# Scores of a windowed attention: every unit by plain float32 products on two row halves of the tensor engine

## The chip, the cores and the metric

The kernel runs on one core of a Trainium2 chip. The metric is the time on the device in microseconds (us). Three runs of the kernel before took 773.89, 774.74 and 775.70 us; their median, 774.74 us, is the number to compare with. Engines are called as the profile calls them: PE (matrix products; PEld is its loading of the stationary operand), DVE (vector engine), ACT (scalar engine with the exponential), POOL (GpSimd) and SP, whose queue issues the DMAs.

## The reference

Attention over 8 batches, 8 heads, 576 positions and 64 columns per head. Half of the heads see the last 32 positions, the other half every fourth of the last 128. The result goes through a maxout FFN with float32 weights that arrive as float64.

```python
scores = scale * np.matmul(q, k.transpose(0, 1, 3, 2))
mask_plain = (rel >= 0) & (rel < window)                                        # window = 32
mask_dil = (rel >= 0) & (rel < window * dilation) & (rel % dilation == 0)       # dilation = 4
scores = np.where(masks[None, :, :, :], scores, -1000000000.0)
scores = scores - np.max(scores, axis=-1, keepdims=True)
attn = np.exp(scores)
attn = attn / (np.sum(attn, axis=-1, keepdims=True) + 1e-09)
attn_out = np.matmul(attn, v)
...
x = np.ascontiguousarray(attn_out.transpose(0, 2, 1, 3)).reshape(B * S, H * D)  # 4608 x 512
h = np.maximum(np.maximum(x @ w1, x @ w2), x @ w3)                              # 4608 x 768
return h @ w_out                                                                # 4608 x 512
```

## The kernel before

**Units.** Attention is cut into 64 units: a half of a sequence (288 queries) for two heads. A unit has 6 blocks (plain heads: 3 per head, 96 queries against up to 128 keys) or 8 blocks (dilated heads: 4 per head, 72 queries against 72 or 104 keys). Blocks of one head lie beside each other, so each block needs only the keys of its window.

**Two ways to the scores.** A score needs float32 accuracy, and the kernel has it in two ways.

- The first 12 units (`LEAN`, line 30) use plain float32 products (line 524). The stationary operand is one head's queries in one half of the 128 rows, with zeros in the other half (`qpads`, line 312); the moving operand is both heads' keys, one under the other. Each such instruction of the program stands as two records in the trace, as every plain float32 product does (also those of line 684).
- The other 52 units split queries and keys into a high and a low part of the type float32r, whose products stand as one record each. A copy makes the high part (`F<-raw`, ACT, line 325), two subtractions the low parts of the queries and of the keys (`F<-raw,F`, POOL or DVE, line 332). High and low queries lie one above the other in the 128 rows; the keys, high and low beside each other, are the moving operand (line 533), so a block of 128 keys has 256 columns. The two halves of the result are summed in two DVE steps: the mask is added to the first half (`masked`, lines 546 and 550, for two blocks at once where they have the same shape), and the second half to that, with the row's maximum taken along (`summed`, line 560). With plain products `masked` is not there, and `summed` takes the scores and the mask.

**From scores to the FFN's input.** ACT takes the exponential of each block and the sum of each row (line 566), POOL adds the small constant (line 621), DVE takes the reciprocal (line 626), POOL multiplies (`W<-W,sm`, line 332). For the first 8 units the tensor engine transposes the probabilities (line 651) and ACT copies them to `PT`; after that DVE transposes (line 672, six steps of a unit). The products with the values (line 684, `pv`) put the two heads of a unit in the two column halves of the tensor engine, in turns. ACT copies `pv` to `xH` as the high part, and DVE subtracts to get the low part `xL`.

**FFN.** 12 tiles of 384 tokens. Each has 18 up products' groups (`u`, line 729: 12 products of 384 columns each, from high and low parts) whose three-way maximum DVE and ACT take (`tmp`), and 3 groups of down products (`d`, line 784: 18 products of 512 columns). `x` is a ring of three tiles; new attention may write a part of it when the tile that reads it has finished its up products.

**Weights.** 24 blocks of up weights and 12 of down weights are converted from float64 words near the start, with three DVE steps for each (`c`, lines 397, 400 and 408).

**Buffers.** The 8 PSUM banks are: 2 for scores (`s`), 1 for transposes (`pt`), 2 for `pv`, 3 for the FFN (line 302). The padded queries take 4 of the 6 buffers of the down weights (`wd`) until the first 12 units are through; staged weights use the others.

**Order.** A planner (`Plan.order`, line 147) lays out all steps by rough costs and due times before anything is issued. Each engine then runs its instructions strictly in that order, and waits where data or a buffer is not there. So an edit of costs, buffers or steps can move instructions on every engine.

## Time and profile before

| what | value |
|---|---|
| median of three runs | 774.74 us (773.89 to 775.70) |
| profiled execution: span from first to last instruction | 775.4 us |
| PE busy, share of the span | 730.6 us, 94% |
| DVE, ACT, POOL busy | 482.5, 384.0, 406.4 us |
| DMA moved | 72.75 MB |
| first FFN product starts | 49.0 us |
| second FFN tile starts | 132.1 us |
| last scores, last `pv` | before 659 us, at 617.6 us |

The page gives no other time of the profiled execution than its span, which lies within the three runs' times and 0.7 us above their median. "Busy" of PE counts an instruction until its result is out, and so overlaps with the next one: how fast products follow each other is read from their starts. Three stretches are to be told apart: the start (to 49 us, attention of the first 8 units and the first weights), the first FFN tile (to 132 us), and the rest.

### The profile page before, as it was taken

The numbers are of one execution on the slowest core, as the hardware profiler recorded it, in microseconds if no ns is written. First come the engines' busy times: TensorE is split into PE (matmuls) and PEld (weight loads), VectorE is DVE, ScalarE is ACT, GpSimd is POOL, SyncE is SP. The second block draws the span as 40 slices with busy tenths as digits, with TensorE's granted clock in tenths as the row PEclk, the third lists the DMA queues.
The fourth block names the chain that finished last, engine by engine and source line by source line (L and its number), as shares of the span: only waits on it lengthen the run. The fifth ranks groups of instructions, "written<-read, shape, count | busy, mean of one in ns | idle before, by whom it ended". The sixth has DMA issues, their size and how long they took to land.

```text
span 775.4 us, 14660 instructions
## 1 busy us (share of the span) xinstructions
PE 730.6 (94%) x4724; PEld 670.2 (86%) x4724; DVE 482.5 (62%) x1865; ACT 384.0 (50%) x1324; POOL 406.4 (52%) x560
## 2 busy tenths in 40 slices
PE   6787589999999999999999999999999999999998
PEld 5676578998998899799799799899699799899996
DVE  6899998888988879643884887511895611011110
ACT  7666466776766667552566477511465211111111
POOL 5877676787788588671288288611176011011110
PEclk9779898999999999999999999999999999999999
DMA  6974144344444433330433342410330200100001
GB/s 192 283 240 145 47 128 135 99 132 135 122 126 134 131 103 107 120 94 23 127 92 96 121 138 66 129 31 1 95 115 33 71 14 0 41 1 14 28 1 41
DMA packets 41516, 72.75 MB, mean 94 GB/s; under 512 B 4320, under 2 KB 15584, under 8 KB 41440
## 3 DMA queue, kind: packets, MB, share of 16 engines
q1 hardware_dynamic: 41440, 71.81, 30.3%
q8 instruction: 38, 0.62, 0.3%
q14 instruction: 38, 0.31, 0.1%
HBM read 62.36 MB, written 9.44 MB: 93 GB/s over the span
## 4 chain that ended last, share of the span: by engine, by line
PE 74%; DVE 19%; issue 3%; DMA 2%; POOL 1%; ACT 1%; SPq 0%; ACTq 0%; POOLq 0%; DVEq 0%
PE u L729 49%; PE d L784 15%; DVE PT L672 5%; PE s L533 5%; PE pv L684 3%; DVE c L408 3%; DVE c L400 3%; DVE W L560 2%; PE s L524 2%; DVE F L332 1%; DVE tmp L332 1%; DVE c L397 1%; DVE xL L332 1%; DMA st<-in_w_up_dram 1%; DVE W L546 1%
## 5 line engine op out<-in xcount | busy, mean ns | idle before, releaser
L332 POOL TENSOR_TENSOR F<-raw,F 64x288 fp32r<-64x288 f32 (+3 forms) x192 | 166.1, 867 | 81.2 <-ACT F L325 38.6
L332 DVE TENSOR_TENSOR tmp<-u,tmp 128x384 f32<-128x384 f32 x144 | 79.9, 555 | 203.0 <-PE u L729 200.4
L566 ACT ACTIVATE W<-W,mx 96x128 f32<-96x128 f32 (+3 forms) x448 | 166.5, 373 | 79.0 <-DVE mx L560 78.3
L729 PE MATMUL u<-xH,wupH 128*128 128x384 f32 x864 | 188.5, 339 | 7.2 <-DVE tmp L332 4.9
L729 PE MATMUL u<-xL,wupH 128*128 128x384 f32 x864 | 187.3, 338 | 0.0
L729 PE MATMUL u<-xH,wupL 128*128 128x384 f32 x864 | 186.4, 337 | 0.0
L332 POOL TENSOR_TENSOR h<-tmp,h 128x384 fp32r<-128x384 f32 x72 | 73.7, 1023 | 202.7 <-ACT h L325 201.7
L784 PE MATMUL d<-wdn,h 128*128 128x512 f32 x648 | 163.8, 401 | 0.0
L729 PEld LDWEIGHTS u<-xH,wupH 128*128 128x128 f32 x864 | 152.0, 189 | 11.2 <-DVE tmp L332 6.7
L729 PEld LDWEIGHTS u<-xL,wupH 128*128 128x128 f32 x864 | 152.1, 189 | 0.4
L729 PEld LDWEIGHTS u<-xH,wupL 128*128 128x128 f32 x864 | 151.5, 189 | 0.3
L672 DVE STREAM_TRANSPOSE PT<-W 32x192 f32<-32x192 f32 (+1 forms) x336 | 134.8, 401 | 13.0 <-PE pv L684 7.5
L784 PEld LDWEIGHTS d<-wdn,h 128*128 128x128 f32 x648 | 119.5, 191 | 24.6
L332 POOL TENSOR_TENSOR W<-W,sm 96x384 f32<-96x384 f32 (+2 forms) x127 | 103.5, 830 | 25.0 <-DVE sm L626 22.8
L325 ACT CAST h<-tmp 128x384 fp32r<-128x384 f32 x72 | 36.8, 511 | 131.2 <-DVE tmp L332 131.1
L566 ACT ACTIVATION_READ_ACCUMULATOR W<-W,mx 72x1 f32 (+1 forms) x448 | 84.1, 188 | 0.0
L325 ACT CAST F<-raw 128x576 fp32r<-128x576 f32 (+2 forms) x103 | 72.1, 704 | 18.2 <-DMA raw<-in_qk_d_dram 8.7
L560 DVE CUSTOM_DVE_ANT_0 W<-W,s 96x128 f32<-96x128 f32 (+2 forms) x364 | 76.6, 252 | 1.2
L546 DVE TENSOR_TENSOR W<-s,mask 72x208 f32<-72x208 f32 (+2 forms) x158 | 53.8, 361 | 28.2 <-PE s L533 26.1
L533 PE MATMUL s<-F 128*96 128x256 f32 (+3 forms) x364 | 59.9, 266 | 7.4 <-DVE mx L560 6.5
L533 PEld LDWEIGHTS s<-F 128*72 128x72 f32 (+1 forms) x364 | 47.0, 151 | 20.2 <-DVE mx L560 5.5
L684 PEld LDWEIGHTS pv<-PT,v 104*64 104x64 f32 (+1 forms) x896 | 36.6, 142 | 27.6 <-issue 15.3
(47 smaller groups left out, 502.6 us busy)
## 6 DMA issues: line engine op xcount, KB each, us to landing
raw<-in_qk_d_dram SPq DMA_DIRECT2D x28, 352.0 KB
st<-in_w_up_dram SPq DMA_DIRECT2D x24, 384.0 KB
out_dram<-o SPq DMA_DIRECT2D x36, 256.0 KB
raw<-in_qk_p_dram SPq DMA_DIRECT2D x28, 304.0 KB
raw<-in_qk_p_dram SPq DMA_DIRECT2D x24, 288.0 KB
raw<-in_qk_d_dram SPq DMA_DIRECT2D x24, 288.0 KB
v<-in_v_d_dram SPq DMA_DIRECT2D x32, 208.0 KB
v<-in_v_p_dram SPq DMA_DIRECT2D x32, 192.0 KB
```

The costliest lines, as they stand in the source:

```text
L325: nc.scalar.copy(dst, src)
L332: (nc.vector if eng == "dve" else nc.gpsimd).tensor_tensor(dst, a, b, op=op)
L400: nc.vector.scalar_tensor_tensor(cw(), words()[:, :, 0], 29, cw(), op0=ALU.logical_shift_right, op1=ALU.bitwise_or)
L408: nc.vector.scalar_tensor_tensor(cw(), words()[:, :, 1], 0x80000000, cw(), op0=ALU.bitwise_and, op1=ALU.bitwise_or)
L533: nc.tensor.matmul(bank.t[:nq, 256 * z : 256 * z + 2 * nk], f[:, q0 : q0 + nq], kv[:, :, k0 : k0 + nk], start=True, stop=True,)
L546: nc.vector.tensor_tensor(W3()[:nq, n0 : n0 + 2, mo : mo + nk], s3[:, :, :nk], m, op=ALU.add)
L560: nc.vector.tensor_tensor_reduce(a, x, y, -0.125, 3e38, ALU.add, ALU.min, mx.t[:nq, n : n + 1])
L566: nc.scalar.activation(a, a, AF.Exp, bias=mx.t[:nq, n : n + 1], scale=-1.0, accum_out=sm.t[:nq, n : n + 1])
L672: nc.vector.transpose(PT.t[c : c + 32, : 2 * nb, 32 * i : 32 * i + 32], W3(e)[32 * i : 32 * i + 32, :, c - e : c - e + 32],)
L684: nc.tensor.matmul(pv.t[64 * j : 64 * j + 64, q0 : q0 + nq], v.t[:wk, j, i, :], PT.t[:wk, nb * j + i, :nq], start=True, stop=True,)
L729: nc.tensor.matmul(bank.t[:, :n], wt[:, 3 * f + g, c, :], (xL if xz else xH)[:, c, r0 : r0 + n], start=(m == 0 and c == 0), stop=(m == 2 a ...
L784: nc.tensor.matmul(bank.t, hs[f].t[:, hz, s0 : s0 + 128], wdn[f].t[:, wz], start=(f == 0 and m == 0), stop=(f == NF - 1 and m == 2),)
```

## The change

All 64 units now get their scores from plain float32 products, and none is split. A unit's queries and keys are loaded in one DMA into one buffer: head 0 in rows 0 to 63, head 1 in rows 64 to 127. For each block there are two products of 64 rows, one in each row half of the tensor engine, in turns between the heads, each head with a PSUM bank of its own. The padded queries with their zeros and their four buffers go, as do the casts and subtractions of queries and keys, the `masked` steps, and the second copies of queries and keys in HBM.

PSUM is dealt out anew: 4 banks for scores, which the early transposes share, 1 for `pv`, 3 for the FFN. Input buffers become `qk` x4 and `v` x3. The planner has other costs for `scores`, `summed` and the exponential, and looks for room for all of a step's new buffers at once.

```diff
@@ buffers
-        "raw": (2, [128, HALF + 416], F32),
-        "F": (2, [128, HALF + 2 * 416], F32R),
-        "v": (2, [128, 2, 4, D], F32),
+        "qk": (4, [128, HALF + 416], F32),
+        "v": (3, [128, 2, 4, D], F32),
...
-    BANKS = {"s": 2, "pt": 1, "pv": 2, "ffn": 3}
+    BANKS = {"s": 4, "pv": 1, "ffn": 3}
...
-    qpads = [(buf("wd", f"q{i}", [128, 2 * HALF], F32), []) for i in range(QPADS)]
...
@@ attention
+        kb, v = buf("qk", f"qk{u}"), buf("v", f"v{u}")
+        qsrc, vsrc = qk_src[hf, dil][b, p % 2], v_src[hf, dil][b, p % 2]
+        load = plan.add(
+            {"sp": 0.5}, lambda _: nc.sync.dma_start(out=kb.t[:, :w], in_=qsrc), [], [kb], nbytes=512 * w
+        )
...
+        banks = [buf("s", f"s{u}_{j}") for j in range(2)]
+
+        def scores(_):
+            for i, (q0, _, k0, nk, _) in enumerate(blocks):
+                for j in range(2):
+                    d = slice(64 * j, 64 * j + 64)
+                    nc.tensor.matmul(
+                        banks[j].t[:nq, wk * i : wk * i + nk],
+                        kb.t[d, q0 : q0 + nq],
+                        kb.t[d, HALF + k0 : HALF + k0 + nk],
+                        start=True,
+                        stop=True,
+                    )
+
+        s = plan.add(
+            {"pe": sum(4 * x[3] / 2400 + 0.008 for x in blocks)}, scores, [load], [kb, *banks], rows=96
+        )
...
+                def summed(_, j=j, i=i, n=n, nk=nk, mo=mo):
+                    nc.vector.tensor_tensor_reduce(
+                        W3()[:nq, n, mo : mo + nk],
+                        banks[j].t[:nq, wk * i : wk * i + nk],
+                        mask[:nq, mo : mo + nk],
...
+                t = plan.add({"dve": dve(nk) + 0.15}, summed, [s], [banks[j], W, mx])
+                expd.append(plan.add({"act": act(nk) + 0.33}, expo, [t], [W, mx, sm]))
...
             if not turned:
-                bank = buf("pt", f"pt{u}_{j}")
+                bank = buf("s", f"pt{u}_{j}")
...
@@ planner
+    def room(st, slots):
+
+        new = [b.tag for b in st.bufs if b.slot is None]
+        at = 0.0
+        for tag in set(new):
+            k = new.count(tag)
+            at = max(at, sorted(slots[tag])[k - 1][0] if len(slots[tag]) >= k else 1e9)
+        return at
```

The order of issue changes on all engines. Two places on PE are shown; `u`, `d`, `s` and `pv` are the PSUM tiles of the up products, the down products, the scores and the products with the values, and the numbers behind them are the planner's.

Between up products in the steady stretch, before (line 729 is `u`, line 533 the split scores):

```order
L729 MATMUL u_0_1_4261<-xH,wupH 128x384 x4
L729 MATMUL u_0_1_4261<-xL,wupH 128x384 x4
L533 MATMUL s_0_4279<-F_0_4234 96x192
L533 MATMUL s_0_4279<-F_0_4234 96x256
L729 MATMUL u_0_1_4261<-xH,wupL 128x384 x4
```

and in the changed kernel (line 623 is `u`, line 461 the scores):

```order
L623 MATMUL u_3_1_2810<-xH,wupL 128x384 x4
L461 MATMUL s_0_2833<-qk_2623 96x96
L461 MATMUL s_1_2834<-qk_2623 96x96
L461 MATMUL s_0_2833<-qk_2623 96x128
L461 MATMUL s_1_2834<-qk_2623 96x128
L461 MATMUL s_0_2833<-qk_2623 96x128
L461 MATMUL s_1_2834<-qk_2623 96x128
L623 MATMUL u_3_2_2844<-xH,wupH 128x384 x4
```

A unit's scores were put between FFN products in three or four pieces, each of products over all 128 rows; now all of them stand in one piece, in which the two row halves take turns.

Among the down products, before (line 784 is `d`, line 684 `pv`):

```order
L784 MATMUL d_0_3179<-wdn_1230,h_2_2861 128x512 x3
L684 MATMUL pv_3203<-PT_93,v_2878 64x72 x8
L684 MATMUL pv_3218<-PT_91,v_2969 64x72 x8
L784 MATMUL d_0_3179<-wdn_1287,h_3_2999 128x512 x3
L784 MATMUL d_0_3179<-wdn_1340,h_4_3091 128x512 x3
L784 MATMUL d_0_3179<-wdn_1366,h_5_3186 128x512 x3
L784 MATMUL d_128_3256<-wdn_1125,h_0_2634 128x512 x3
L684 MATMUL pv_3264<-PT_92,v_3228 64x96 x6
```

and in the changed kernel (line 678 is `d`, line 578 `pv`):

```order
L578 MATMUL pv_2328<-PT_93,v_2285 64x72 x8
L678 MATMUL d_256_2341<-wdn_988,h_0_1745 128x512 x3
L678 MATMUL d_256_2341<-wdn_1019,h_1_1855 128x512 x3
L678 MATMUL d_256_2341<-wdn_1109,h_2_1976 128x512 x3
L578 MATMUL pv_2362<-PT_91,v_2254 64x72 x8
L678 MATMUL d_256_2341<-wdn_1157,h_3_2075 128x512 x3
L678 MATMUL d_256_2341<-wdn_1198,h_4_2174 128x512 x3
L678 MATMUL d_256_2341<-wdn_1239,h_5_2238 128x512 x3
L578 MATMUL pv_2395<-PT_92,v_2346 64x72 x8
```

With two banks, two units' `pv` could stand back to back; with one, nine down products stand between them.

More of the change, by code (lines that the diff above doesn't have):

```diff
@@ L166, in order @@
                         continue
[L167 to L169 removed]
+                    if st.bufs:
+                        at = max(at, self.room(st, slots))
                     if best is not None and (at, st.due) >= best[:2]:
@@ L310, in buf @@
         return Buf(work, tag, n, shape or sh, dtype or dt, name)
-    qpads = [(buf("wd", f"q{i}", [128, 2 * HALF], F32), []) for i in range(QPADS)]
-    for qb, _ in qpads:
-        qb.take()
-        for j in range(2):
-            nc.vector.memset(qb.t[64 * j : 64 * j + 64, HALF * (1 - j) : HALF * (2 - j)], 0.0)
     for i, t in enumerate(KEPT["W"]):
@@ L440, in attention @@
         wk = 104 if dil else 128
-        pairs = [(j, i) for j in range(2) for i in range(nb)]
-        lean = u < LEAN
-        Fs, parts = [], []
-        if lean:
-            kb = buf("F" if u % 2 and u < KEYS_F else "raw", f"k{u}", SIZES["raw"][1], F32)
-            qb, qread = qpads[u % QPADS]
-            qk = lean_src[hf, dil][b, p % 2]
-            def load_q(_, j):
-                d = slice(64 * j, 64 * j + 64)
-                nc.sync.dma_start(out=qb.t[d, HALF * j : HALF * j + HALF], in_=qk[d, :HALF])
-            def load_k(_):
-                nc.sync.dma_start(out=kb.t[:, :ksz], in_=qk[:, HALF:w])
-            q0 = plan.add({"sp": 0.5}, lambda _: load_q(_, 0), qread, [qb], nbytes=256 * HALF)
-            kl = plan.add({"sp": 0.5}, load_k, [], [kb], nbytes=512 * ksz)
-            q1 = plan.add({"sp": 0.5}, lambda _: load_q(_, 1), qread, [qb], nbytes=256 * HALF)
-            parts = [[q0, kl], [q1, kl]]
-            Fs = [kb, kb]
-            qread.clear()
@@ L465, in attention @@
-        for j in range(0 if lean else 2):
-            raw, F = buf("raw", f"raw{u}_{j}"), buf("F", f"F{u}_{j}")
-            Fs.append(F)
-            def load(_, raw=raw, j=j):
-                nc.sync.dma_start(out=raw.t[:, :w], in_=qk_src[hf, dil][b, 2 * (p % 2) + j])
-            def qlow(e, raw=raw, F=F):
-                tt(e, F.t[64:, :HALF], raw.t[64:, :HALF], F.t[64:, :HALF].bitcast(F32), ALU.subtract)
-            def klow(e, raw=raw, F=F):
-                tt(e, F.t[:, w : w + ksz], raw.t[:, HALF:w], F.t[:, HALF:w].bitcast(F32), ALU.subtract)
-            s = plan.add({"sp": 0.5}, load, bufs=[raw], nbytes=512 * w)
-            s = plan.add(
-                {"act": act(w), "dve": dve2(w), "pool": pool1(w)},
-                lambda e, raw=raw, F=F: copy(e, F.t[:, :w], raw.t[:, :w]),
-                [s],
-                [raw, F],
-            )
-            parts.append(
-                [
-                    plan.add({"pool": pool(HALF), "dve": dve(HALF)}, qlow, [s], [raw, F]),
-                    plan.add({"pool": pool(ksz), "dve": dve(ksz)}, klow, [s], [raw, F]),
-                ]
-            )
@@ L496, in attention @@
             lambda _: nc.sync.dma_start(out=v.t[: vsrc.shape[0], :, :nb, :], in_=vsrc),
-            [] if lean else [x for pt in parts for x in pt],
+            [],
             [v],
@@ new lines, in attention, with expo @@
+        s = plan.add(
+            {"pe": sum(4 * x[3] / 2400 + 0.008 for x in blocks)}, scores, [load], [kb, *banks], rows=96
+        )
+        for j in range(2):
+            for i in range(nb):
+                n, (nk, mo) = j * nb + i, blocks[i][3:]
+                def summed(_, j=j, i=i, n=n, nk=nk, mo=mo):
[3 more added lines that the diff above has]
+                        mask[:nq, mo : mo + nk],
+                        -0.125,
+                        3e38,
+                        ALU.add,
+                        ALU.min,
+                        mx.t[:nq, n : n + 1],
+                    )
+                def expo(_, n=n, nk=nk, mo=mo):
+                    a = W3()[:nq, n, mo : mo + nk]
+                    nc.scalar.activation(
+                        a, a, AF.Exp, bias=mx.t[:nq, n : n + 1], scale=-1.0, accum_out=sm.t[:nq, n : n + 1]
+                    )
+                t = plan.add({"dve": dve(nk) + 0.15}, summed, [s], [banks[j], W, mx])
+                expd.append(plan.add({"act": act(nk) + 0.33}, expo, [t], [W, mx, sm]))
```

110 lines of the change are left out of this document (4 added, 106 removed).

## The prediction

> **What bounds the kernel now.** I read the page's totals first, then the stretches, then the chain of waits, then single products.
>
> ```profile
> span 775.4 us, 14660 instructions
> PE 730.6 (94%) x4724; PEld 670.2 (86%) x4724; DVE 482.5 (62%) x1865; ACT 384.0 (50%) x1324; POOL 406.4 (52%) x560
> ```
>
> ```profile
> 4.00:40.00 36.00, 28.31 (x254) 24.80 (x254) 27.86 (x164) 25.97 (x128) 23.69 (x43) 0.86 0.87 257
> 40.00:112.00 72.00, 54.85 (x321) 49.87 (x321) 71.59 (x162) 43.06 (x133) 50.94 (x60) 0.88 0.45 143
> 132.00:618.00 486.00, 475.79 (x3213) 436.11 (x3212) 341.93 (x1427) 275.32 (x973) 296.13 (x407) 1.00 0.33 99
> 618.00:659.00 41.00, 41.00 (x232) 40.23 (x232) 6.59 (x12) 6.34 (x13) 5.06 (x5) 1.00 0.02 7
> ```
>
> The columns are the stretch, its length, busy PE, PEld, DVE, ACT and POOL, then the granted clock. DVE is full from 40 to 112 us (71.59 of 72), and what fills it are the weights:
>
> ```profile
> L408 DVE SCALAR_TENSOR_TENSOR c<-st,c 128x384 uint32<-128x384 uint32 (+1 forms) x34 | 28.0, 823 | 0.1
> L400 DVE SCALAR_TENSOR_TENSOR c<-st,c 128x384 uint32<-128x384 uint32 (+1 forms) x35 | 24.9, 711 | 0.1
> L397 DVE TENSOR_SCALAR c<-c 128x384 uint32<-128x384 uint32 (+1 forms) x35 | 20.7, 593 | 0.0
> ```
>
> From 132 us to the end PE is the bound: 475.79 of 486, then all of it, at clock 1.00. So the change has to be costed twice: on DVE in the first 132 us, on PE after that. Relief of POOL and ACT counts only where PE waits for them.
>
> The last tiles have no attention, and price the FFN (start, length, what):
>
> ```profile
> 659.66 12.38 PE d L784 x54
> 672.04 37.44 PE u L729 x216
> 771.72 0.58 ACT o L325
> ```
>
> A tile is 37.44 + 12.38 = 49.8 us, one up product 37.44 / 216 = 0.173, and the span ends 3.7 us after the last product.
>
> The products around attention, from PE's timeline (start, length, instructions):
>
> ```profile
> 16.22 0.74 PE L524 MATMUL s<-k,q 128*72 128x72 f32 x8
> 132.13 0.86 PE L729 MATMUL u<-xH,wupH 128*128 128x384 f32 x4
> 132.83 0.54 PE L533 MATMUL s<-F 128*72 128x208 f32 x4
> 133.21 0.53 PE L729 MATMUL u<-xL,wupH 128*128 128x384 f32 x2
> 205.60 0.86 PE L729 MATMUL u<-xH,wupL 128*128 128x384 f32 x4
> 206.39 0.72 PE L684 MATMUL pv<-PT,v 104*64 104x72 f32 x16
> 207.04 0.97 PE L729 MATMUL u<-xH,wupH 128*128 128x384 f32 x4
> 245.10 1.22 PE L684 MATMUL pv<-PT,v 104*64 104x72 f32 x32
> 396.94 0.63 PE L533 MATMUL s<-F 128*96 128x256 f32 x4
> 397.41 0.88 PE L729 MATMUL u<-xH,wupL 128*128 128x384 f32 x4
> ```
>
> - **Split scores** cost (397.41 - 396.94) / 4 = 0.118 us for a block of 128 keys, (133.21 - 132.83) / 4 = 0.095 for 104: 0.00092 a key. Nothing is lost at their edges. A unit has on average 2 x 360 keys: 0.66 us.
> - **Products in two halves of the array** can be seen in `pv`, whose heads lie in the two column halves. 32 records took 1.22, 16 took 0.72, so 16 cost 0.50: a pair of 72 columns every 0.0625 us. Eight records of the same 72 columns over the whole array take 0.74. So 16 half-array records go through in the time of 8 whole ones: two halves run together.
> - **Changing to halves and back** costs time. From 205.60 to 207.04 are 1.44 us; four up products are 0.69 of it, the `pv` products 0.50; 0.25 us is left, once per group.
>
> Behind 132 us the trace has so many of them:
>
> ```profile
> 132.00:659.00 527.00, 56.91 (x352) 44.87 (x352) 1.00 0.31 92
> 132.00:659.00 527.00, 34.73 (x716) 27.80 (x716) 1.00 0.31 92
> ```
>
> The first row is line 533, the second line 684. 352 score products are 50.3 units, 716 records of `pv` 51.1 units. The order of issue has these `pv` in 38 groups. So the 643.3 us from 132.1 to 775.4 are: FFN 11 x 49.8 = 548.0, end 3.7, scores 50.3 x 0.66 = 33.2, `pv` 51.1 x 0.50 = 25.6, changes 38 x 0.25 = 9.4, together 619.9. The other **23.4 us are waits** of PE, and they are what the lighter DVE, ACT and POOL can give back.
>
> **The change part by part.**
>
> *Scores on PE.* Unit for unit the new products stand in pairs, 0.0625 us for two records of 72 columns; by columns that is 0.61, 0.67, 0.50 and 0.72 us for the four kinds of unit, on average 0.625 against 0.66. The trace shows column halves, not row halves; the bounds of a pair are 0.0625 and 0.125 (one after the other). I take 0.0625, since `pv` is the same float32 product with its two halves in turns and a tile of PSUM rows for each, as here a bank for each.
>
> The Trainium skill, "TensorE: Matmul & The Clock Gate", Part 3, has four row tiles at 3.07 times the speed of one, not four. Scaled to two that is 1.54 times, an estimate; the scores behind the first tile would then cost 38.2 us instead of 29.4, and the forecast would be 781. The `pv` row, at 0.50 for 16, shows no such loss for column halves.
>
> *Changes of the array's shape.* Every score group now stands between products over the whole array (the order has `u`, six or eight scores, `u`), so it should pay what a `pv` group pays. Bounds: 0, as the split scores pay now, and 0.25, the `pv` group. I take 0.25, since a group in halves is nearer to `pv`. Counted in the new order from the second tile on: 47 score groups (17 units are done by then, 14 before the change), 50 `pv` groups, and 14 borders at which scores and `pv` touch and half a change (0.12) is saved.
>
> New sum behind the first tile: 548.0 + 3.7 + scores 47 x 0.625 = 29.4, `pv` 50 x 0.50 = 25.0, `pv` changes 50 x 0.25 = 12.4, score changes 47 x 0.25 = 11.6, less 1.7: 628.4 us without waits, 8.5 more than the 619.9 of before.
>
> *Waits.* What leaves the other engines in this stretch:
>
> ```profile
> L332 POOL TENSOR_TENSOR F<-raw,F 64x288 fp32r<-64x288 f32 (+3 forms) x181 | 155.8, 862 | 78.8 <-ACT F L325 36.6 <-issue 30.5 <-POOL W L332 2.7
> L325 ACT CAST F<-raw 128x576 fp32r<-128x576 f32 (+2 forms) x98 | 68.6, 703 | 17.2 <-DMA raw<-in_qk_d_dram 8.7 <-PE s L533 7.3 <-POOL W L332 0.5
> L546 DVE TENSOR_TENSOR W<-s,mask 72x208 f32<-72x208 f32 (+2 forms) x152 | 51.5, 360 | 28.1 <-PE s L533 26.1
> L550 DVE TENSOR_TENSOR W<-s,mask 96x96 f32<-96x96 f32 (+1 forms) x48 | 10.6, 263 | 4.3 <-PE s L533 4.1
> L332 DVE TENSOR_TENSOR F<-raw,F 64x288 fp32r<-64x288 f32 (+1 forms) x16 | 16.3, 1020 | 1.5 <-ACT F L325 1.1
> ```
>
> DVE loses 51.5 + 10.6 + 16.3 = 78 of 342 us, ACT 69 of 275, POOL 156 of 296. The waits of PE that the trace names are mostly for DVE and its banks:
>
> ```profile
> PE s L533 <- DVE mx L560: 5.7, 7, 1.5
> PE pv L684 <- PE pv L684: 2.1, 3, 0.7
> ```
>
> With four score banks and a DVE busy for 264 of 486 us I take two thirds of the 23.4 us away: 8 stay. Bounds: 0 and 23.4. From the second tile on this makes 628.4 + 8 = 636.4 against 643.3: **-6.9 us**.
>
> *The start.* Its units were lean already, so DVE is spared no `masked` here. By the new order DVE has, up to the last maximum of the first tile: 7 copies of `PT`, one more cast to `xH` and two to `wupH` that it takes over, one more `xL`, 5 more transposes, 5 more `summed`, one more `c` and reciprocal; it loses 8 memsets of padded queries.
>
> ```profile
> L329 DVE CAST xH<-pv 128x288 fp32r<-128x288 f32 x1 | 0.4, 443 | 0.0
> L672 DVE STREAM_TRANSPOSE PT<-W 32x192 f32<-32x192 f32 x11 | 4.0, 367 | 0.2
> L316 DVE MEMSET q<- 64x288 f32 x8 | 2.4, 298 | 1.6 <-PEq L884 0.9
> ```
>
> Ten copies and casts at 0.44, `xL` at 0.45, transposes 5 x 0.37, `summed` 5 x 0.25, `c` and reciprocal 0.8, less 2.4: +6.4 us. DVE idles for 36.0 - 27.9 = 8 us between 4 and 40 us, and the new order has its first weights earlier there; I let 4 of the 6.4 go into that idle time (bounds 0 and 6.4): +2.4. Behind the last maximum PE has, beside the same `d`, one `pv` group more (0.75) and three score groups with changes (2.6) for 18 split products (1.7): +1.7. Together **+4.1 us**.
>
> *DMA* moves fewer bytes and lies at 0.33 of its engines behind 132 us; the loads of the first 8 units are 0.3 MB each as before. I cost it at nothing; the cover is four buffers of `qk`.
>
> Sum: 775.4 + 4.1 - 6.9 = 772.6 for the span. It lies 0.7 above the median of 774.74, so **772 us**.
>
> **The rivals.**
>
> 1. *The row halves don't run together.* Then each of 47 units pays 0.625 more: +29.4, **801 us**; half-way 787. Against it: the `pv` rows. Chance 0.10.
> 2. *The single `pv` bank stalls PE.* It ends slower. A `pv` may only start when ACT has made `xH` and DVE `xL` from the one before:
>
> ```profile
> 245.87 0.90 ACT L325 CAST xH<-pv 128x288 fp32r<-128x288 f32 x2
> 247.24 0.45 DVE L332 TENSOR_TENSOR xL<-pv,xH 128x288 fp32r<-128x288 f32 x1
> 374.84 0.72 PE L684 MATMUL pv<-PT,v 128*64 128x96 f32 x12 [0.67 <-PE pv L684]
> ```
>
> From the cast's start at 245.87 to the end of `xL` at 247.69 are 1.8 us here, while nine down products give 2.08 (12.38 / 54 x 9). It decides once the chain is over 2.1 us long; a wait like the 0.67 at 374.84, at 0.4 on average for some 35 groups among down products, gives +14: **786 us**. Against it: 1.0 us of those 1.8 is DVE at six transposes, and DVE gets lighter. Chance 0.12.
>
> 3. *The start grows.* If none of the 6.4 us is hidden (+4) and PE, with half as much to do in its first 40 us, is granted a lower clock than 0.86 there, and each unit's chain starts some 3 us later: **779 us**. Chance 0.12.
> 4. *Score groups change shape for nothing*, as split scores do: -11.6, **760 us**, and 752 with no waits left. Chance 0.18.
>
> **How the numbers follow.** My forecast has 0.48 and its own range is 767 to 777, by a few us of waits and of the start either way. What a measurement here can tell from no change is 0.2%, 1.5 us: faster is below 773.2, slower above 776.3. Faster: 0.30 of the forecast's 0.48, all of rival 4, 0.03 of rival 3: 0.51. Same: 0.12 + 0.02 of rival 3 + 0.01 of rival 2: 0.15. Slower: 0.06 + 0.10 + 0.11 + 0.07: 0.34. The range for 8 in 10 reaches from rival 4 to rival 2, 760 to 787; it leaves out whole serial products and the best of rival 4.
>
> **What would show it.** Score records in pairs a few ns apart, 16 of 72 columns in 0.50 us, show the halves together; 1.0 us shows rival 1. From the last up product ahead of a score group to the first behind it, 0.17 + 0.25 + the group's own time shows the change of shape. The second tile's first up product should start near 136 us; 140 is rival 3. `pv` waiting for `pv` among the down products, over 5 us in all, is rival 2. The clock should stay at 1.00 behind the first tile; if it falls there, all of this is wrong.

## The result, and the profile after

The changed kernel is a little **slower**: 781.24 us in the median of 8 runs (779.80 to 783.14), the kernel before beside it 775.38 (773.89 to 779.74). The ratio is 1.0063 with a 95% interval of 1.0046 to 1.0080. The forecast was 772 with faster as the likeliest sign; 781 lies in the range, but the sign was wrong.

The page of the changed kernel, its span, the engines and the chain of waits:

```profile
span 779.7 us, 14321 instructions
PE 738.9 (95%) x5088; PEld 665.8 (85%) x5088; DVE 404.8 (52%) x1642; ACT 315.9 (41%) x1210; POOL 244.3 (31%) x371
PE 89%; DVE 5%; POOL 2%; issue 2%; DMA 1%; SPq 0%; ACT 0%; POOLq 0%
```

The other engines did get lighter: DVE from 482.5 to 404.8 us, ACT from 384.0 to 315.9, POOL from 406.4 to 244.3. PE is busy for 8 us more. The stretches (length, busy PE, PEld, DVE, ACT, POOL, granted clock, DMA share, GB/s):

```profile
4.00:40.00 36.00, 24.42 (x233) 19.21 (x232) 26.04 (x155) 24.33 (x122) 26.26 (x43) 0.76 0.88 305
40.00:112.00 72.00, 51.80 (x312) 47.07 (x312) 69.90 (x156) 36.58 (x104) 46.25 (x53) 0.74 0.38 119
138.70:659.00 520.30, 518.40 (x3713) 467.81 (x3710) 269.93 (x1178) 214.66 (x866) 141.72 (x224) 1.00 0.19 59
```

Behind the first tile PE is now busy for 518.40 of 520.30 us; before it was 475.79 of 486. So the waits did go, and PE filled the time with something else. In front of it the clock is lower (0.76 and 0.74 against 0.86 and 0.88) and DVE is as full as before from 40 to 112 us.

The second tile's first up product, from PE's timeline (start, length, instructions), is at 138.7 us instead of 132.1:

```profile
138.73 0.97 PE L623 MATMUL u<-xH,wupH 128*128 128x384 f32 x4
```

So the profiled execution loses 6.6 us in front of that product and gains 2.3 behind it (779.7 - 138.7 = 641.0 against 643.3). The prediction had +4.1 and -6.9.

A caution on these differences: wherever a run has both its time and its span on record, the time is 1.7 to 2.2 us longer, mostly 1.8. So the profiled execution of the kernel before, with its span of 775.4, took some 777.2 us. That is above its three runs, not among them, and 1.8 above the median of 775.38; the changed kernel's profiled execution took 781.49, only 0.25 above its median. The two profiles lie 4.3 us apart where the medians lie 5.9 apart, so what is compared with the trace of before is known to some 2 us.

A score group in the steady stretch, from the same view:

```profile
161.09 0.86 PE L623 MATMUL u<-xH,wupL 128*128 128x384 f32 x4
161.88 0.74 PE L461 MATMUL s<-qk 64*72 64x72 f32 x16
162.55 0.97 PE L623 MATMUL u<-xH,wupH 128*128 128x384 f32 x4
163.36 0.85 PE L623 MATMUL u<-xL,wupH 128*128 128x384 f32 x4
```

From 161.09 to 162.55 are 1.46 us: four up products 0.69, 16 score records 0.50 to 0.52, and 0.25 for the change of shape, as predicted. But the next four up products take from 162.55 to 163.36, 0.81 us instead of 0.69. The cost of the change doesn't end with the first product behind the group. The kernel before shows it behind its `pv` group too; its row after the 207.04 that the prediction quoted is:

```profile
207.85 0.86 PE L729 MATMUL u<-xL,wupH 128*128 128x384 f32 x4
```

207.85 - 207.04 is again 0.81. The whole change is therefore 0.25 + 0.12 = 0.37 us by these rows. I call it **theory A**: a change of the array's shape costs some 0.36 us (0.25, and 0.11 for the second product, its mean over all groups), not 0.25.

The named waits of PE behind 138.7 us are these two rows; before they came to 10 us:

```profile
PE pv L578 <- PE d L678: 1.3, 3, 0.5
PE pv L578 <- issue: 0.4, 2, 0.2
```

### The profile page after: what moved, and what is told of

The parts are those of the page before. It is cut to its first block, busy times and chain, and to the rows that moved or that the text cites. A ratio compares the mean times of both kernels' runs of the same rounds, so it can differ in the third digit from the quotient of the medians.

```text
span 779.7 us, 14321 instructions
## 1 busy us (share of the span) xinstructions
PE 738.9 (95%) x5088; PEld 665.8 (85%) x5088; DVE 404.8 (52%) x1642; ACT 315.9 (41%) x1210; POOL 244.3 (31%) x371
## 4 chain that ended last, share of the span: by engine, by line
PE 89%; DVE 5%; POOL 2%; issue 2%; DMA 1%; SPq 0%; ACT 0%; POOLq 0%
PE u L623 58%; PE d L678 20%; PE s L461 6%; PE pv L578 5%; DVE c L393 2%; DVE c L401 1%; POOL W L325 1%; DVE c L390 1%; DMA st<-in_w_up_dram 1%; POOL c L385 1%; DVE xL L325 0%; SPq L442 0%; POOL sm L515 0%; SPq L438 0%; DVE PT L322 0%
## 5 line engine op out<-in xcount | busy, mean ns | idle before, releaser
L623 PE MATMUL u<-xL,wupH 128*128 128x384 f32 x864 | 190.2, 341 | 0.5 <-DVE xL L325 0.5
L490 ACT ACTIVATE W<-W,mx 96x128 f32<-96x128 f32 (+2 forms) x448 | 166.2, 374 | 24.6 <-DVE mx L477 24.2
L678 PE MATMUL d<-wdn,h 128*128 128x512 f32 x648 | 160.4, 397 | 0.0
L623 PEld LDWEIGHTS u<-xH,wupL 128*128 128x128 f32 x864 | 154.4, 190 | 1.6 <-issue 0.2
L477 DVE CUSTOM_DVE_ANT_0 W<-s,mask 96x128 f32<-96x128 f32 (+2 forms) x448 | 90.3, 251 | 4.2 <-issue 2.8
L461 PE MATMUL s<-qk 64*96 64x128 f32 (+3 forms) x896 | 61.3, 274 | 6.4 <-DMA qk<-in_qk_p_dram 3.7
L461 PEld LDWEIGHTS s<-qk 64*72 64x72 f32 (+1 forms) x896 | 48.3, 161 | 21.4 <-issue 9.3
L578 PE MATMUL pv<-PT,v 104*64 104x72 f32 (+1 forms) x896 | 50.1, 255 | 13.5 <-issue 5.9
L318 ACT COPY tmp<-u 128x384 f32<-128x384 f32 x72 | 34.5, 480 | 58.8 <-PE u L623 56.9
L318 ACT COPY o<-d 128x512 f32<-128x512 f32 x36 | 21.1, 586 | 76.0 <-PE d L678 75.8
## 6 DMA issues: line engine op xcount, KB each, us to landing
st<-in_w_up_dram SPq DMA_DIRECT2D x24, 384.0 KB
```

The costliest lines, as they stand in the source:

```text
L318: nc.scalar.copy(dst, src)
L461: nc.tensor.matmul(banks[j].t[:nq, wk * i : wk * i + nk], kb.t[d, q0 : q0 + nq], kb.t[d, HALF + k0 : HALF + k0 + nk], start=True, stop=True,)
L477: nc.vector.tensor_tensor_reduce(W3()[:nq, n, mo : mo + nk], banks[j].t[:nq, wk * i : wk * i + nk], mask[:nq, mo : mo + nk], -0.125, 3e38, ...
L490: nc.scalar.activation(a, a, AF.Exp, bias=mx.t[:nq, n : n + 1], scale=-1.0, accum_out=sm.t[:nq, n : n + 1])
L578: nc.tensor.matmul(pv.t[64 * j : 64 * j + 64, q0 : q0 + nq], v.t[:wk, j, i, :], PT.t[:wk, nb * j + i, :nq], start=True, stop=True,)
L623: nc.tensor.matmul(bank.t[:, :n], wt[:, 3 * f + g, c, :], (xL if xz else xH)[:, c, r0 : r0 + n], start=(m == 0 and c == 0), stop=(m == 2 a ...
```

## The experiments

Every kernel ran four times or more, beside the kernel before. "Runs" counts the unbroken runs of half-array products (scores, `pv`, or both side by side) between whole-array ones, from the second tile on, in the order of issue; in the changed kernel, e2, e3 and e6 the first of them stands just ahead of the tile's first product. "Second tile" is the start of its first up product and "behind" the span less that start, both from the profiled execution. Kernels with the same order up to there (changed, e13, e14) start the second tile at 138.5 to 139.3 us, so differences of the start below 0.8 us say nothing.

| kernel | edit of the changed kernel | runs | second tile | behind | median | ratio to before (95%) |
|---|---|---|---|---|---|---|
| before | | | 132.1 | 643.3 | 775.38 | 1 |
| changed | none | 84 | 138.7 | 641.0 | 781.24 | 1.0063 (1.0046 to 1.0080) |
| e1 | two units' scores in one group | 66 | 148.7 | 631.9 | 782.99 | 1.0088 (1.0062 to 1.0114) |
| e2 | a unit's scores in two groups | 116 | 141.4 | 652.3 | 795.02 | 1.0236 (1.0210 to 1.0262) |
| e3 | early scores issued twice | 84 | 138.6 | 640.9 | 783.57 | 1.0090 (1.0059 to 1.0122) |
| e4 | the planner's old costs | 72 | 141.2 | 639.3 | 782.18 | 1.0077 (1.0048 to 1.0107) |
| e5 | staging buffers held back | 85 | 136.0 | 641.9 | 779.25 | 1.0044 (1.0027 to 1.0060) |
| e6 | 3 banks `s`, 2 `pv` | 86 | 133.8 | 646.0 | 780.16 | 1.0061 (1.0045 to 1.0076) |
| e7 | padded products for 12 units | 85 | 157.8 | 638.5 | 797.93 | 1.0288 (1.0272 to 1.0303) |
| e8 | e7 and pairs from unit 13 on | 62 | 179.6 | 626.6 | 807.85 | 1.0414 (1.0398 to 1.0430) |
| e9 | transposes in a bank `ffn` | 87 | 134.6 | 644.4 | 780.50 | 1.0043 (1.0028 to 1.0058) |
| e10 | e5 and pairs from unit 13 on | 69 | 132.9 | 635.1 | **769.07** | **0.9899 (0.9884 to 0.9913)** |
| e11 | e9 and e10 | 63 | 162.6 | 626.7 | 791.36 | 1.0185 (1.0170 to 1.0200) |
| e12 | e5 and pairs from unit 17 on | 70 | 135.9 | 635.5 | 773.20 | 0.9956 (0.9938 to 0.9973) |
| e15 | the banks of before | 90 | 137.2 | 648.1 | 789.86 | 1.0171 (1.0154 to 1.0188) |
| e16 | pairs from unit 13 on | 70 | 134.6 | 635.5 | 772.64 | 0.9950 (0.9931 to 0.9969) |

e13 and e14 change the last tile alone and are told with their own numbers; their medians are 789.80 and 797.48 us (ratios 1.0170 and 1.0264).

### More and fewer changes of shape (e1, e2)

e1 issues the scores of two neighbouring units in one group from the ninth unit on, so that half of the score groups go:

```diff
-        def scores(_):
-            for i, (q0, _, k0, nk, _) in enumerate(blocks):
+            def scores(_):
+                for kb, _, banks in mine.values():      # units u and u + 1
+                    for i, (q0, _, k0, nk, _) in enumerate(blocks):
```

> From the ninth unit on, the scores of two units stand in one group; the products are the same ones. Behind the first FFN tile the order then has 23 score groups instead of 47. Theory A (each group in row halves between whole-array products costs 0.36 us of change: 0.25 up to the first product behind it, and 0.11 more because the second product behind it is late): 24 x 0.36 less, a little of it lost on borders with pv that no longer touch, so 7 to 8 us less than the changed kernel, 773 to 774. Theory B (the changed kernel is slower for its score products or for waits, not for the changes of shape): within 2 us of 781, or slower, since a pair needs all four score banks at once.

e2 goes the other way, two groups for each unit:

```diff
+        parts = [range(2), range(2, nb)] if u >= 8 else [range(nb)]
+        for part in parts:
+            s = plan.add({"pe": ...}, lambda e, part=part: scores(e, part), [load, s], [kb, *banks], rows=96)
```

> From the ninth unit on, a unit's scores are issued in two groups, the second after the first has begun to be read; the products are the same ones. Behind the first FFN tile the order has 86 score groups instead of 47. Theory A: 39 x 0.36 = 14 us more, less 1 to 2 for new borders with pv: 792 to 794. Theory B: within 2 us of 781, or faster, since banks are read sooner.

Behind the first tile both did what theory A says. e2 has 32 more runs and is 11.3 us longer there, 0.2 of which are two more score products behind the tile's start: 11.1 / 32 = 0.35 us for each. e1 has 17 fewer runs behind the tile's first product and is 9.1 us shorter; 1.2 of that are products (one unit's scores and one unit's `pv`) moved ahead of it, which leaves 7.9 / 17 = 0.46, with six places fewer where scores and `pv` touch.

The price can also be read from the traces group by group: from the last whole product ahead of a group to the eighth behind it, less the products' own time, in groups with no wait of PE. In the changed kernel 33 groups of scores alone cost 0.39 us in the mean and 31 of `pv` alone 0.38; the 69 such groups of e2 and the 55 of e1 cost 0.38. The 12 runs of the changed kernel in which scores and `pv` touch cost 0.50 to 0.55.

e1 still lost, because of its start, which I had not seen coming. PE's waits there:

```profile
PE pt L560 <- DVE mx L492: 21.1, 2, 18.8
PE pv L593 <- DVE xL L325: 8.6, 2, 5.7
```

A pair takes all four score banks at once. PE runs its instructions in order, and it stands for 18.8 us at a transpose, whose result needs one of these banks, until DVE has read the scores out of it (line 492).

### The price by itself (e13, e14)

The last tile has no attention. e13 issues two products of 72 columns there, one in each row half, behind each of the 18 groups of up products; e14 issues eight. Their results are not used, and no other instruction of PE moves.

```diff
+                        for i in range(1 if m == 2 and spare else 0):      # e14: range(4)
+                            for j in range(2):
+                                d = slice(64 * j, 64 * j + 64)
+                                nc.tensor.matmul(
+                                    spare[j].t[:72, 72 * i : 72 * i + 72],
+                                    KEPT["PT"][0][d, 0, :72], KEPT["PT"][0][d, 1, :72], start=True, stop=True)
```

> The changed kernel, whose order stays as it is, with two more products of 72 columns (one in each row half, 0.125 us together) behind each of the 18 groups of up products of the last tile, which has no attention; their results are not used. Theory A (0.36 us for each change of the array's shape, the late second product with it): 18 x (0.125 + 0.36) = 8.7 us more in that tile. The prediction's 0.25: 18 x (0.125 + 0.25) = 6.8 us more. Rival 4 of the prediction (the change is free): 2.3 us more.

> As e13_extra1 with eight products (four in each row half, 0.50 us together) instead of two. Theory A: 18 x (0.50 + 0.36) = 15.5 us more in the last tile than in the changed kernel, and 6.8 more than in e13_extra1. The prediction's 0.25: 13.5 more. If the row halves did not run together: 18 x (1.0 + 0.25) = 22.5 or above.

The last tile in the chain of waits of the changed kernel (start, length, what):

```profile
726.52 37.44 PE u L623 x216
763.97 12.27 PE d L678 x54
```

of e13, its first and its last groups:

```profile
726.31 2.08 PE u L624 x12
728.40 0.28 PE x L634 x4
728.68 2.31 PE u L624 x12
...
772.49 0.28 PE x L634 x4
772.77 12.47 PE d L689 x54
```

and of e14:

```profile
727.13 2.08 PE u L624 x12
729.22 0.67 PE x L634 x16
729.89 2.29 PE u L624 x12
...
779.54 0.67 PE x L634 x16
780.21 12.48 PE d L689 x54
```

From the tile's start to the first down product are 37.45 us in the changed kernel, 46.46 in e13 and 53.08 in e14. With the 0.2 us by which the down products take longer that is 9.2 and 15.8 us more, or 0.51 and 0.88 for each of the 18 places. Taking off 0.125 and 0.50 for the products leaves **0.39 and 0.38 us** for a change of shape, whether one pair of products stands there or four. The 12 more records of e14 cost 0.37 a place, 0.061 for a pair of records: the two row halves run together without loss. The prediction's 0.25 would have been 6.8 and 13.5 us.

PE's timeline of e13 shows where the 0.38 lies:

```profile
745.69 0.86 PE L624 MATMUL u<-xH,wupL 128*128 128x384 f32 x4
746.48 0.35 PE L634 MATMUL x<-PT 64*72 64x72 f32 x4
746.76 0.97 PE L624 MATMUL u<-xH,wupH 128*128 128x384 f32 x4
747.57 0.88 PE L624 MATMUL u<-xL,wupH 128*128 128x384 f32 x4
```

The first half-array product comes 0.10 us late (0.79 instead of 0.69), the first whole one behind it 0.15 (0.28 less 0.125), and among the next four products another 0.12 is lost. The Trainium skill, "TensorEngine Tiling (Array Packing)", Key Properties, says that a change of tiling mode drains the engine, and gives no price. The trace shows a price, 0.38 us to the halves and back; it doesn't show whether a drain makes it up.

One rival to the shape is the type of the numbers: scores and `pv` are plain float32, the FFN's products float32r. The kernel before has a group of plain float32 products over all 128 rows (the padded queries, line 524) between up products, with no wait of PE:

```profile
99.60 0.86 PE L729 MATMUL u<-xH,wupH 128*128 128x384 f32 x4
100.30 0.68 PE L524 MATMUL s<-k,q 128*72 128x72 f32 x8
100.78 0.95 PE L729 MATMUL u<-xL,wupH 128*128 128x384 f32 x4
101.57 0.86 PE L729 MATMUL u<-xH,wupL 128*128 128x384 f32 x4
```

From 99.60 to 101.57 are 1.97 us. Eight up products are 1.39 of it, and the eight records, whose starts are 0.065 us apart, 0.52: some 0.06 us is left, where a group in halves leaves 0.37 or more. This is a single group, but it speaks for the shape and against the type.

### What makes the start late: the clock, the costs, the staging (e3, e4, e5)

e3 issues the score products of the first 12 units twice, so that PE is busier in its first 40 us and may be granted a higher clock:

```diff
-            for i, (q0, _, k0, nk, _) in enumerate(blocks):
+            for i, (q0, _, k0, nk, _) in [*enumerate(blocks)] * (2 if u < 12 else 1):
```

> The first 12 units issue every score product twice, the second time over the first result; the order of issue of everything else is that of the changed kernel. Theory C (the first FFN tile starts 9 us later because the tensor engine, with half as much score work, is granted half its clock from 32 to 67 us): the granted clock between 30 and 67 us rises, the first FFN product comes 3 to 6 us sooner than 58 us, and the time falls to 775 to 778. Theory D (the start is late by its order on the vector engine, whatever the clock): the first FFN product stays at 58 us or comes later, the time is 781 to 785.

Its first stretches:

```profile
4.00:40.00 36.00, 27.33 (x358) 23.00 (x356) 28.45 (x156) 24.30 (x122) 25.68 (x44) 0.89 0.88 305
40.00:112.00 72.00, 54.36 (x355) 49.83 (x355) 69.28 (x157) 36.57 (x105) 45.41 (x53) 0.75 0.39 119
```

The clock of the first stretch rose from 0.76 to 0.89, above that of the kernel before, and the second tile still started at 138.6. So the lower clock of the first 40 us is not what makes the start late. In the second stretch the clock stayed at 0.75; what a higher clock there would bring isn't shown.

e4 gives the planner its old costs of `summed` and of the exponential:

```diff
-                t = plan.add({"dve": dve(nk) + 0.15}, summed, [s], [banks[j], W, mx])
-                expd.append(plan.add({"act": act(nk) + 0.33}, expo, [t], [W, mx, sm]))
+                t = plan.add({"dve": dve(nk) + 0.01}, summed, [s], [banks[j], W, mx])
+                expd.append(plan.add({"act": act(nk) + 0.15}, expo, [t], [W, mx, sm]))
```

> Only the planner's costs of the masked sum and of the exponential are those of the kernel before (0.01 and 0.15 instead of 0.15 and 0.33). Theory D (the new costs make the planner put weights and copies ahead of attention on the vector engine at the start): the first FFN product comes 4 to 9 us sooner than 58 us and the time is 774 to 777. Theory C: the first FFN product stays within 2 us of 58. Behind the first tile the order has 38 score groups instead of 47, which by theory A alone is 3 us less, 778.

The first up product came 2.4 us sooner, at 55.9, but the second tile started at 141.2 instead of 138.7, later and not earlier. The planner also put 26 more score products and 16 more of `pv` ahead of that tile, so the old costs don't bring the old start back, but what the costs alone do isn't shown.

e5 keeps weights out of four of the six staging buffers until the first 12 units have their scores, as the padded queries did before:

```diff
+    held = [buf("wd", f"q{i}", [128, 2 * HALF], F32) for i in range(4)]      # taken at the start
...
-            {"sp": 0.5}, lambda _: nc.sync.dma_start(out=kb.t[:, :w], in_=qsrc), [], [kb], nbytes=512 * w
+            {"sp": 0.5}, lambda _: nc.sync.dma_start(out=kb.t[:, :w], in_=qsrc), [], [kb, *hb], nbytes=512 * w
```

> Four of the six buffers in which weights are staged are kept from them until the first 12 units have their scores, as the padded queries did before; nothing is written there, and the scores stay in row halves. Theory E (the freed buffers let weights in early, and their conversion runs ahead of attention on the vector engine and POOL): the first FFN product comes at 49 to 53 us instead of 58, the second tile at 131 to 134 instead of 138.5, the time is 774 to 777. If staging has nothing to do with it: 57 to 59 us, 138, 780 to 783.

This took 2.7 us off the start and left the stretch behind it nearly as it was (641.9). So one part of the late start is that the padded queries' buffers went to the weights, which the diff doesn't show as a change to the weights at all.

### What makes the start late: the banks (e6, e9, e15)

The waits of PE in the first 132 us, in the kernel before

```profile
PE pv L684 <- issue: 8.3, 2, 6.2
PE s L524 <- DVE mx L560: 6.4, 5, 2.5
```

and in the first 140 us of the changed one:

```profile
PE pt L545 <- DVE mx L477: 7.9, 3, 4.6
PE pv L578 <- issue: 5.5, 2, 4.5
PE pv L578 <- DVE xL L325: 5.3, 2, 2.7
PE pt L545 <- POOL W L325: 4.4, 4, 2.1
```

The first and the third row are new, and both are PSUM: transposes now share the score banks and wait for DVE to read scores, and the single `pv` bank waits for DVE's `xL`. The fourth row is new too.

What DVE does meanwhile is weights. Ahead of the first up product, at 58.3 us instead of 49.0, PE has the same products in both kernels (152 records of scores, 112 of `pv`, 56 of transposes), but its named waits there are 24.9 us against 14.2. DVE's weight steps (`c`) up to that product, in the changed kernel and before (stretch, length, busy, clock, DMA share, GB/s):

```profile
0.00:58.30 58.30, 25.75 (x39) 0.69 0.73 246
0.00:49.00 49.00, 18.72 (x30) 0.83 0.81 237
```

The last `pv` of the changed kernel ahead of it waits for the `xL` of the unit before:

```profile
56.66 0.45 DVE L325 TENSOR_TENSOR xL<-pv,xH 128x288 fp32r<-128x288 f32 x1
57.16 1.23 PE L578 MATMUL pv<-PT,v 104*64 104x72 f32 x16 [2.61 <-DVE xL L325]
```

This `xL` is the seventh. Up to the fifth (41.7 us, and 40.0 before) DVE has done 18 and 20 weight steps, up to the seventh (56.7 and 49.6) 35 and 30. So most of the lateness arises between the two, where the planner now has 17 weight steps on DVE instead of 10. Which part of the edit made it order them so isn't separated.

e6 deals the banks out otherwise, e9 puts the transposes into FFN banks, which are idle then, and e15 goes back to the banks of before:

```diff
-    BANKS = {"s": 4, "pv": 1, "ffn": 3}
+    BANKS = {"s": 3, "pv": 2, "ffn": 3}                # e6
+    BANKS = {"s": 2, "pt": 1, "pv": 2, "ffn": 3}       # e15, with the transposes in "pt"
...
-                bank = buf("s", f"pt{u}_{j}")
+                bank = buf("ffn", f"pt{u}_{j}")        # e9
```

> Three score banks and two pv banks instead of four and one. Theory G (the single pv bank holds the tensor engine up, at the start, where it waits 5 us for xL, and among the down products): the first FFN product comes 3 to 5 us sooner than 58 us, the stretch behind the first tile is 2 to 4 us shorter (45 pv groups instead of 51), the time is 774 to 777. If the bank is no hindrance, a third score bank that a unit cannot use alone costs waits: 781 to 785.

> The changed kernel, with the results of the first eight units' transposes in a bank of the kind "ffn", idle until the first up product, instead of one of the four that the scores now share with them. Theory H (the start is late because a transpose, which TensorE takes in order, stands until VectorE, busy with the weights, has read scores out of the bank that it needs: waits of 7.9, 4.6 and 3 us at transposes in the changed kernel): with the bank always free the second tile starts near 133 us instead of 138.5, the stretch behind it stays at 641 with its 48 groups of scores, and the time is 775 to 777. Rival I (VectorE itself is what is late, and the banks only show where TensorE stands meanwhile): the wait goes to the next score group or the next product of values, the second tile starts at 137 to 140, and the time is 780 to 783.

> The changed kernel with the PSUM banks of the kernel before: 2 for scores, 1 for the early transposes, 2 for values, 3 for the FFN. Theory B (sharing the score banks with the transposes and the single bank for values are what makes the start later than before): the second tile starts at 132 to 134 us, against 138.5 in the changed kernel and 131.9 before. Rival (staging, which e5_hold showed to take 2.7 us, is needed too): 135 to 137. Behind it 49 groups of scores and 45 of values with 4 borders between them, 90 changes of shape instead of 84, and waits for the two score banks: 645 to 650 us. The time is 778 to 783.

e6 and e9 brought the second tile forward by 4.9 and 4.1 us, so the banks are a part of the late start, though one unit's scores fewer stand ahead of it in both (224 records instead of 236). In e9 the wait of the transposes for DVE is gone; the two largest waits are now

```profile
PE pv L578 <- issue: 10.9, 4, 3.1
PE pt L545 <- POOL W L325: 5.4, 4, 2.1
```

But neither made the kernel faster by as much. The stretch behind grew by 5.0 us in e6 and by 3.4 in e9. In e9 one more unit's scores and two more units' `pv` stand behind the second tile's first product (1.7 us of products, in 4 more runs), which is 1.7 + 4 x 0.38 = 3.2 of the 3.4. In e6 the named waits of PE there grew from 1.7 to 5.1 us. A start that is shorter covers less attention, and what isn't covered comes back at PE's full price.

e15 fell short of what I had expected of the banks: the second tile started at 137.2, which is the rival's 135 to 137 and not 132 to 134. The wait for DVE's maxima only went back to the score products, and longer than before:

```profile
PE s L461 <- DVE mx L477: 10.7, 6, 3.2
PE pt L545 <- ACT PT L318: 7.0, 4, 3.8
```

The time, 789.86 us, was also above the 783 expected (the profiled execution, at 787.11, was the fastest of its four). The banks of before are therefore not all that the start lacked.

### Going back for the first units (e7, e8)

e7 gives the first 12 units the padded products of the kernel before, inside the new buffers and banks; e8 adds pairs from the thirteenth unit on. Both also plan the scores of those 12 units with their buffer `W` in hand, and the loads of the later units behind the scores of the fourth unit before.

```diff
-                        kb.t[d, q0 : q0 + nq],
-                        kb.t[d, HALF + k0 : HALF + k0 + nk],
+                        qb.t[:, HALF * j + q0 : HALF * j + q0 + nq] if lean else kb.t[d, q0 : q0 + nq],
+                        kb.t[slice(None) if lean else d, HALF + k0 : HALF + k0 + nk],
```

> The first 12 units have their scores from padded queries over all 128 rows, as before the change, with their buffers; a unit's scores are planned with its buffer W in hand, so that banks are not held without it. All other units stay in row halves. If the start of the changed kernel is late for anything that comes with those 12 units (staging, the clock, the order): the first FFN product at 48 to 53 us, the second tile at 131 to 134, and, with 42 score groups instead of 47 behind it, 771 to 775. If it is late for the new bank and planner costs alone: 56 to 59 us, 779 to 782.

> The padded first 12 units and, from the thirteenth on, the scores of two units in one group: 21 score groups behind the first tile. By theory A for the steady stretch (632 us there in the run with pairs, 641 in the changed kernel) and a start like that of before (132 us): 764 to 768, faster than both kernels. If the start stays at 138 or later: 770 or more.

Both missed by far in the start, at 157.8 and 179.6 us. Behind the tile e8 has 62 runs and takes 626.6 us, again as theory A says. Going back to padded products for the first units did not bring the old start back; both starts were worse. As these edits move the order on every engine, they don't show what the row halves of the first units cost alone.

### Both remedies together (e10, e11, e12, e16)

> The changed kernel with four of the six staging buffers of the weights held back from them until the first twelve units have their scores (as alone in e5_hold), and from the thirteenth unit on the scores of two units in one group (in e1_pairs from the ninth). Theory A (a change of the array's shape with its late second product costs 0.36 us, whatever the order): 24 groups of scores behind the first tile instead of 47, so 632 to 634 us behind it instead of 641.9; with the second tile at 136 as in e5_hold the time is 770 to 772. Rival (two units' scores in one group hold up the tensor engine wherever they stand, since four banks must be free at once and the second tile's products wait behind them): a start of 140 or more or a rest of 638 or more, and 777 to 783.

> e9_ptbank and e10_held_pairs12 together. The planner then puts 152 instead of 112 score products ahead of the second tile and 16 instead of 12 groups of values, 7 us of tensor work more there, and leaves 21 groups of scores and 47 of values behind it. By theories A and H the stretch behind is 626 us, the second tile starts at 138 to 140 (133 and the work moved there), and the time is 766 to 770. By rival I the start is 145 or more and the time 773 to 778.

> e10_held_pairs12 with pairs from the seventeenth unit on only, so that the first tile has the order of e5_hold but for its last two score groups. Theory A: 24 groups of scores behind the first tile, 632 to 634 us there; the second tile starts at 135.5 to 136.5 as in e5_hold; 770 to 771. Rival (pairs hold up the tensor engine wherever they stand): a rest of 638 or more, 777 or more.

> e10_held_pairs12 without the held buffers: the changed kernel with the scores of two units in one group from the thirteenth unit on. Theory A: 24 groups of scores behind the first tile, 634 to 636 us there; the second tile starts at 135 to 138, 1 to 3 us later than in e10_held_pairs12; 771 to 774 us. Rival (the pairs hold the start up without the held buffers, as in e1_pairs): 145 or more and 780.

The edits are those of e1 (with `u >= 12` or `u >= 16` in place of `u >= 8`), e5 and e9. **e10 beats both kernels**: 769.07 us, 1.0% under the kernel before. Its last tiles stand as they did, 12 us earlier:

```profile
714.81 37.44 PE u L643 x216
752.25 12.27 PE d L698 x54
```

Against e5 it has 16 fewer runs and is 6.8 us shorter behind the tile, although 1.2 us more of products stand there. The second tile starts at 132.9, 3.1 us earlier; those products, one unit's scores and one unit's `pv`, are a part of that. The rest of 635.1 is above the 632 to 634 expected. e16 shows that the pairs alone give 772.64, and holding the staging buffers back the other 3.6 us. e12's 773.20 is above its expected 771: its start of 135.9 was as expected, its rest of 635.5 above the 632 to 634. Pairs from the ninth unit on (e1) cost 10 us in the start, from the thirteenth on none: in the order of e1 the first pair stands ahead of the last 24 transposes of PE, in that of e10 all transposes are issued before the first pair.

e11 went further off than either theory had it; the second tile starts at 162.6 us. PE's waits:

```profile
PE pv L598 <- DVE xL L329: 19.6, 3, 10.9
PE s L474 <- DVE mx L497: 14.0, 4, 10.3
```

The planner, with more banks free early, put 152 instead of 112 score products ahead of the second tile, and PE stands there for DVE's maxima and its `xL`. The wait for DVE shows a third time, at yet other instructions.

## Why the prediction was wrong, step by step

- **The two stretches, and their bounds, held.** PE at clock 1.00 sets the time behind the first tile (518.40 of 520.30 us), and DVE is full ahead of it (69.90 of 72).
- **The row halves run together: right.** 0.061 us for a pair of 72 columns (e13 against e14), 0.0625 predicted from `pv`'s column halves. Rival 1, at 801, is out, and so is the estimate from the Trainium skill, "TensorE: Matmul & The Clock Gate", Part 3, of 38.2 us for the scores instead of 29.4.
- **"Changes of the array's shape" is the step that failed.** The prediction took 0.25 us from 205.60 to 207.04, and as its upper bound. It stopped at the first product behind the group; the next row would have shown another 0.12. Measured by itself it is 0.38. With that, the terms 12.4 + 11.6 - 1.7 = 22.3 (90 changes by the prediction's count) become 34.2, and its sum without waits 640.3 instead of 628.4. In the kernel before, the 38 `pv` changes grow from 9.4 to 14.4 and the sum from 619.9 to 624.9. The scores in halves thus cost PE 15.4 us more behind the first tile, not 8.5. The changed kernel's own trace bears the 34.2 out: its 76 runs that can be read clear of waits cost 30.9 us, and the other seven at the same price make it 33.7. With this term alone put right, the forecast of -2.8 us for the span turns into +4.1, or 779.5 us: the step decides the sign. That this comes so close to the measured 779.7 is luck: the start came out 2.5 us dearer and the waits 2.3 us cheaper than forecast, which nearly cancels.
- **The waits: the size was about right, the reason only in part.** Of the 23.4 us that the prediction called waits, 5.0 were this same cost, which leaves 18.4. Of these the trace names 10.0 as waits of PE. Some 3.5 are whole products that follow late behind the split score groups, at whose edges the prediction saw nothing lost; its row at 397.41 is followed by this one, after 0.72 us instead of 0.69:

```profile
398.13 0.86 PE L729 MATMUL u<-xH,wupH 128*128 128x384 f32 x4
```

The other 4.9 stand in no row. In the changed kernel 641.0 - 640.3 = 0.7 is left, against the 1.7 that the trace names. So 17.7 us came back where the prediction took 15.4, but lighter engines are shown for the named waits alone, 10.0 - 1.7 = 8.3 of them. Together: +15.4 - 17.7 = -2.3, the difference between the two profiles.
- **"The start" had the sign right and the size wrong**: +6.6 instead of +4.1, nearer to rival 3's 140 us for the second tile than to the forecast's 136. The prediction added up steps that DVE gains. What the trace shows instead is weight steps that the planner put ahead of the last attention steps (35 instead of 30 up to the seventh `xL`), and PE waiting behind them; from 4 to 40 us DVE is even less busy than before (26.04 against 27.86). Buffers and banks changed hands: e5 takes 2.7 of the 6.6 us, e9 4.1 and e6 4.9, and they don't add up. Rival 3 had the later start but put it on DVE's added work and the lower clock; e3 shows that it isn't the clock of the first 40 us. The other parts of its 4 us were not tested apart.
- **Rival 2** (the single `pv` bank stalls PE among the down products) is out: all named waits there come to 1.7 us where over 5 were to show it, and a second bank (e6) left the stretch behind the tile 5 us longer. What the single bank costs shows in the start, at the `pv` of 57.16 us, which waits 2.61 us.
- **Rival 4** (score groups change shape for nothing) had 0.18 and is out: e13 measures 0.39 us where it has none. Its evidence, the split scores, used the whole array.

**What stays open.** Why PE, in every order that was tried, reaches the second tile no earlier than before, at best at 132.9 us (e10), isn't settled: the traces show weight steps of DVE ahead of what PE waits for, not why the planner puts them there. The banks of before (e15) and the held buffers (e5) each leave a part, and both together were not tried with single groups. All these starts come from a planner that lays all engines out anew with each edit, and the experiments show where PE waits, not which order would be best.

## What to carry to other kernels

Price a change of the array's shape from a whole product ahead of the group to the second one behind it, and multiply by the number of groups before the products inside them are counted: here 47 groups at 0.38 us (17.9 us) ate up the 17.7 us that came back elsewhere, 8.3 of them named waits. If the products themselves are cheap, make the groups fewer and longer, as the pairs in e10 did, but only from where nothing else needs the banks that a long group takes. And when a buffer goes, ask who gets it: four staging buffers given to the weights cost the start 2.7 us though no step of the weights was touched.

## What the runs showed of the hardware that I had not expected

A change between the whole array and its row halves and back costs 0.38 us, in three parts: 0.10 on the way in, 0.15 ahead of the first whole product and 0.12 among the next four. It didn't depend on whether two or eight products stood between (0.39 and 0.38). Plain float32 products over all 128 rows, in the one group that could be read, left 0.06 us. The two row halves together lose nothing: 0.061 us for two records of 72 columns, as the column halves of `pv` had it with 0.0625.
